# Full-width weight windows for the routing's counting and id products

## The chip, the core and the metric

The kernel runs on one core of one Trainium2 chip. Its time is the device time of one execution in microseconds (us), the median over several runs. A core has five engines with queues of their own: TensorE (PE in the profile; its weight loads are listed apart as PEld), VectorE (DVE), ScalarE (ACT), GpSimd (POOL) and SyncE (SP, which only issues transfers here). TensorE multiplies a stationary operand, which a weight load (LDWEIGHTS) brings into its array of 128 rows and 128 columns, with a moving operand, and writes the sums to PSUM.

## The reference

The input is the output of three layers, one after the other.

```python
attn = softmax(mask(q @ k.T / 8)) @ v        # 4 batches, 8 heads, 576 positions, window of 64 back
x = attn.reshape(2304, 512)

logits = x @ w_gate                          # 2304 tokens, 8 experts, cap = 288 per expert
for idx in np.argsort(-logits.flatten()):    # best pair of token and expert first
    tok, e = divmod(idx, 8)
    if assigned[tok] < 0 and counts[e] < 288:
        assigned[tok] = e; counts[e] += 1
y[mask_e] = relu(x[mask_e] @ w1[e]) @ w2[e]  # for each expert e

h = y @ w_in                                 # 512 -> 2048
out = maximum(0.01 * h, h) @ w_out           # 2048 -> 512
```

## The kernel before

Attention comes first (to about 87 us of the span). Then the greedy assignment is made in eight phases, 0 to 7, one for each expert that fills up. A phase looks for the logit at which the first expert reaches 288 tokens: six rounds of a search (r = 0 to 5) over the bits of the logit, each with J = 63 or 31 candidate thresholds. In a round VectorE compares each token's best logit with all candidates and writes the one-hot-like grid `GE` (128 partitions, 18 chunks of tokens, J columns, bf16). TensorE then counts: 18 small products, one per chunk, with `GE[:, c, :J]` stationary and the one-hot choice `OH[:, c]` (8 columns) moving, all adding into one PSUM tile `pc` with the counts of candidate j in row j. VectorE marks in `sat` which counts have reached the rest (`rem`), and one product with a constant 128x128 matrix `pow2[r]` sums the marked bits over the rows for all partitions. After the six rounds VectorE makes a running count (`W`, the scan `S`), two products with `tri` and `ones` turn it into positions, and 18 more products, with 36 columns of the grid `OB` stationary, give the list of token ids of this expert. So a phase has 6 x 18 counting products and 18 id products on TensorE; I call each such row of 18 a burst. Phase 7 has no search.

Phase 0 runs alone between attention and the first expert. Phases 1 to 6 are cut into small pieces and strewn among the products of the experts (tiles `h`, `ya`, moving 288 columns) and of the last two layers (tiles `h`, `oa`, moving 512 columns), in an order that a planner (`RouteDriver` with the cost table of `Clocks`) fixes when the program is built. Its cost of a product depends on the moving width alone. All these operations are issued through one helper, so the profile gives them one line, L1178; they are told apart by tile names: `rp<-r_oh,r_ge` is a counting product, `rp<-r_lo,r_ob` an id product, `rp<-r_sat,pow` the product behind a round, `rp<-r_tot` the two behind the scan.

The lines that matter (`start`/`stop` arguments left out; the first is in every round, the last at a phase's end):

```python
GE = t([128, NT, 64], BF, "ge", f"{ph}_{r}")
nc.tensor.matmul(pc[:J], GE[:, c, :J], OH[:, c, :])
TT(out=self.sat[:J], in0=pc[:J], in1=(self.rem0 if r == 0 else self.rem)[:J], op=ALU.is_ge)
nc.tensor.matmul(pa, self.pow2[r], self.sat)
nc.tensor.matmul(pi, OB[:, c, :2].rearrange("p a b -> p (a b)"), LO[:, c])
```

Of the kernel before, what the change touches and what calls it, by code (L numbers as in the profile page):

```python
# [58 lines left out]
def attention(nc, tc, ident, identb, qT, kT, v, vT, wg_sb, maskb, xd, L, filler, early, late, done):  # L59


    with ExitStack() as ctx:
# [208 lines left out]
def consts_np():  # L271

    f, i, b = {}, {}, {}
    p = np.arange(128, dtype=np.float32)[:, None]
    u = (np.arange(1, 64, dtype=np.uint64) << 26).astype(np.uint32)
    t = np.where(u >= 0x80000000, u ^ np.uint32(0x80000000), ~u).astype(np.uint32)
    i['t1'] = np.broadcast_to(t.view(np.int32), (128, 63))
    for r, (s, n) in enumerate(zip(SHIFTS, NB)):
        i[f'jt{r}'] = np.broadcast_to((np.arange(1, n + 1) << s).astype(np.int32), (128, n))
    f['ew'] = np.broadcast_to(8 - np.arange(8, dtype=np.float32), (128, 8))  # L280
    f['lim'] = np.where(p == 0, -1.0, 3e9).astype(np.float32)
    f['cid'] = np.broadcast_to(np.arange(18, dtype=np.float32), (128, 18))
    f['pid'] = np.broadcast_to(p, (128, 1))
    f['cont'] = np.broadcast_to((np.arange(288) % NT > 0).astype(np.float32), (128, 288))
    f['ident'] = np.eye(128, dtype=np.float32)
    j = np.arange(128)[:, None] % 18
    f['comb'] = (np.where(p < 18, 128, 1) * (j // 6 == np.arange(3))).astype(np.float32)
    b['mask'] = const_mask()
    b['ident'] = np.eye(128, dtype=np.float32)
    b['tri'] = (p < np.arange(128)[None, :]).astype(np.float32)  # L290
    b['iota'] = np.broadcast_to(np.arange(512, dtype=np.float32) % 128, (128, 512))
    b['spread'] = (j % 6 == np.arange(96) // 16).astype(np.float32)
    b = {k: (np.ascontiguousarray(a).view(np.uint32) >> 16).astype(np.uint16) for k, a in b.items()}
    return f, i, b
# [9 lines left out]
class Router:  # L304
# [3 lines left out]
    def __init__(self, nc, pool, pp, L, cf, ci, cb, ones_b, pow2):  # L308
        self.nc, self.pool, self.pp = nc, pool, pp
        self.cf, self.ci, self.tri, self.iota, self.ones, self.pow2 = cf, ci, cb['tri'], cb['iota'], ones_b, pow2  # L310
        self.Lm, self.nps = L, 0
        self.base = pool.tile([128, 2, 8], F32, name="r_base")
        self.uw = pool.tile([128, 8], F32, name="r_uw")
        self.slotg = pool.tile([128, NT], F32, name="r_slotg")
        self.rem = pool.tile([128, 8], F32, name="r_rem")
        self.rem0 = pool.tile([128, 8], F32, name="r_rem0")
        self.spread = cb['spread']
        self.sat = pool.tile([128, 8], BF, name="r_sat")
        self.ip = pool.tile([128, 128], F32, name="r_ip")
    def start(self):  # L320
        v, cf = self.nc.vector, self.cf
# [11 lines left out]
    def t(self, shape, dt, name, ph):  # L333
        bufs = {"fb": 2, "ns": 2, "T": 2, "U": 2, "ids": 8, "eidx": 8}.get(name, 1)
        return self.pool.tile(shape, dt, tag="r_" + name, name=f"r_{name}_{ph}", bufs=bufs)
    def ahead(self, a, b):

        v = self.nc.vector
        if a == 0:
            self.first = [self.t([128, NT], F32, "m", 0), self.t([128, NT, 8], BF, "oh", 0), self.t([128, NT], F32, "mxw", 0)]  # L340
            self.ge0 = self.t([128, NT, 64], BF, "ge", "0_0")
            self.eqw0 = self.t([128, NT, 8], F32, "eqw", 0)
        m, OH, mxw, eqw = self.first[0][:, a:b], self.first[1][:, a:b], self.first[2][:, a:b], self.eqw0[:, a:b]
        def b3(ap, last):
            return ap.unsqueeze(2).to_broadcast([128, b - a, last])
        def bm(ap, last):
            return ap.unsqueeze(1).to_broadcast([128, b - a, last])
        v.tensor_reduce(out=m, in_=self.Lm[:, a:b], axis=AX.X, op=ALU.max)
        yield True
        v.tensor_tensor(out=eqw, in0=self.Lm[:, a:b], in1=b3(m, 8), op=ALU.is_equal)  # L350
        yield True
        v.tensor_tensor(out=self.ge0[:, a:b, :63], in0=b3(m, 63), in1=bm(self.ci['t1'].bitcast(F32), 63), op=ALU.is_ge)
        v.tensor_tensor(out=eqw, in0=eqw, in1=bm(self.cf['ew'], 8), op=ALU.mult)
        yield True
        v.tensor_reduce(out=mxw, in_=eqw, axis=AX.X, op=ALU.max)
        yield True
        v.tensor_tensor(out=OH, in0=eqw, in1=b3(mxw, 8), op=ALU.is_equal)
    def phase(self, ph, out):

        nc, t = self.nc, self.t
        v, cf, ci = nc.vector, self.cf, self.ci
        Lm = self.Lm
        TT, TS, STT = v.tensor_tensor, v.tensor_scalar, v.scalar_tensor_tensor
# [4 lines left out]
        if ph:  # L370
# [8 lines left out]
            OH = t([128, NT, 8], BF, "oh", ph)  # L379
            TT(out=OH, in0=eqw, in1=b3(mxw, NT, 8), op=ALU.is_equal)  # L380
            yield 'd', 0
        else:
            m, OH, mxw = self.first
        theta = None
        if ph < 7:
            fb = ns = U = None
            T = ci['t1']
            for r in range(6):
                J = 63 if r == 0 else NB[r - 1]
                GE = self.ge0 if ph + r == 0 else t([128, NT, 64], BF, "ge", f"{ph}_{r}")  # L390
                pc = None
                for lo, hi in () if ph + r == 0 else ((0, 9), (9, 18)) if J > 32 or ph == 0 else ((0, 18),):
                    w = hi - lo
                    TT(out=GE[:, lo:hi, :J], in0=b3(m[:, lo:hi], w, J), in1=bm(T.bitcast(F32), w, J), op=ALU.is_ge)
                    if hi == 9:
                        yield 'p' if ph == 0 else 'd', 0
                        if ph == 0:
                            pc = self.ps(64, 8)
                            for c in range(9):
                                nc.tensor.matmul(pc[:J], GE[:, c, :J], OH[:, c, :], start=(c == 0), stop=False)  # L400
                if r >= 2:
                    nf = t([128, 1], I32, "fb", f"{ph}_{r}")
                    TT(out=nf, in0=fb, in1=ns, op=ALU.bitwise_xor)
# [4 lines left out]
                    TT(out=U[:, :Jn], in0=ci[f'jt{r}'], in1=fb.to_broadcast([128, Jn]), op=ALU.bitwise_xor)  # L408
                yield 'p', 0
                c0 = 9 if pc is not None else 0  # L410
                pc = self.ps(64, 8) if pc is None else pc
                for c in range(c0, NT):
                    nc.tensor.matmul(pc[:J], GE[:, c, :J], OH[:, c, :], start=(c == 0), stop=(c == NT - 1))
                yield 'v', 1
                TT(out=self.sat[:J], in0=pc[:J], in1=(self.rem0 if r == 0 else self.rem)[:J], op=ALU.is_ge)
                yield 'p', 0
                pa = self.ps(128, 8)
                nc.tensor.matmul(pa, self.pow2[r], self.sat, start=True, stop=True)
# [3 lines left out]
                if r == 0:  # L422
                    k = t([128, 2], I32, "k", ph)
# [13 lines left out]
        ge = t([128, 2, NT], F32, "gteq", ph)  # L437
# [4 lines left out]
        else:  # L442
# [2 lines left out]


        yield 'd', 0
        W = t([128, 2, 8, NT], BF, "ge", f"{ph}_W")
        TT(out=W, in0=OH.rearrange("p c e -> p e c").unsqueeze(1).to_broadcast([128, 2, 8, NT]),
           in1=ge.unsqueeze(2).to_broadcast([128, 2, 8, NT]), op=ALU.mult)  # L450
        S = t([128, 2, 8, NT], F32, "ob", f"{ph}_S")
        v.tensor_tensor_scan(S.rearrange("p k e c -> p (k e c)"), cf['cont'], W.rearrange("p k e c -> p (k e c)"), 0.0, ALU.mult, ALU.add)
        yield 'd', 0
        tot = t([128, 16], BF, "tot", ph)
        v.tensor_copy(tot.rearrange("p (k e) -> p k e", k=2), S[:, :, :, NT - 1])
# [49 lines left out]
        TS(out=hl[:, 0], in0=loc, scalar1=4, scalar2=None, op0=ALU.arith_shift_right)  # L505
        TS(out=hl[:, 1], in0=loc, scalar1=15, scalar2=None, op0=ALU.bitwise_and)
        yield 'd', 0
        OB = t([128, NT, 3, 18], BF, "ob", ph)
        LO = t([128, NT, 16], BF, "lo", ph)
        TT(out=OB[:, :, 2], in0=b3(hl[:, 0], NT, 18), in1=bm(self.iota[:, :18], NT, 18), op=ALU.is_equal)  # L510
        yield 'd', 0
# [2 lines left out]
        TT(out=OB[:, :, 0], in0=OB[:, :, 2], in1=b3(cf['cid'], NT, 18), op=ALU.mult)  # L514
        TS(out=OB[:, :, 1], in0=OB[:, :, 2], scalar1=cf['pid'], scalar2=None, op0=ALU.mult)
        yield 'p', 0
        pi = self.ps(36, 16)
        for c in range(NT):
            nc.tensor.matmul(pi, OB[:, c, :2].rearrange("p a b -> p (a b)"), LO[:, c], start=(c == 0), stop=(c == NT - 1))
        yield 'v', 1  # L520

        TT(out=self.ip[:36, :96].rearrange("p (a b) -> p a b", a=6), in0=pi.unsqueeze(1).to_broadcast([36, 6, 16]), in1=self.spread[:36].rearrange("p (a b) -> p a b", a=6), op=ALU.mult)
        yield 'p', 0
        pj = self.ps(128, 3)
        nc.tensor.matmul(pj, self.ip, cf['comb'], start=True, stop=True)
# [16 lines left out]
def make_pow2(nc, pool):  # L542
    out = []
    for r, (s, n) in enumerate(zip((25,) + SHIFTS, (63,) + NB)):
        w = pool.tile([128, 128], BF, name=f"pow2_{r}", tag=f"pow2_{r}")
        nc.gpsimd.memset(w, 0.0)
        nc.gpsimd.memset(w[:n], float(1 << s))
        out.append(w)
    return out

# [813 lines left out]
```

## Time and profile before

| what | value |
|---|---|
| time, median of 3 runs | 797.8 us (797.09 to 800.81) |
| time of the profiled execution | 801.13 us |
| span of its instructions | 798.9 us |
| TensorE busy | 757.1 us, 95% of the span |
| VectorE busy | 436.9 us, 55% |
| ScalarE busy | 340.4 us, 43% |
| share of the chain that ended last: TensorE | 60% |
| of it, products that write the tile `rp` | 4% |
| mean granted clock of TensorE | 0.975 of full speed |

The table is read from the page of the profile: its first part gives busy times, its fourth the chain of work that ended last, followed back from the end. Busy time of TensorE runs from the start of a product to its modelled end, so products that follow each other overlap, and what a product costs is seen in the distance between starts, not in its duration.

### The profile page before, as it was taken

To read this page: it belongs to the slowest core of one execution; us is meant where nothing else is said; L and a number is where in the kernel's file an instruction comes from. 1 tells how busy PE (TensorE), PEld (TensorE's weight loads), DVE (VectorE), ACT (ScalarE), POOL (GpSimd) and SP (SyncE) were. 2 spreads that over 40 slices of the span, in tenths; PEclk is the share of its full clock that TensorE was granted. 3 is DMA by queue.
4 is the path that set the end of the run, shared out by engine and by line. 5 is a ranking of instruction groups with operands and counts; after the bars stand their busy time and mean duration, and the time that the engine had idled before them with its cause. 6 is when DMAs were issued, how large, how long until landed. Compare 5 with 4: busy or idle time off the path is not lost.

```text
span 798.9 us, 15084 instructions
## 1 busy us (share of the span) xinstructions
PE 757.1 (95%) x5829; PEld 632.8 (79%) x5829; DVE 436.9 (55%) x1191; ACT 340.4 (43%) x754; POOL 143.0 (18%) x174
## 2 busy tenths in 40 slices
PE   6999659899999999999999999999999999999996
PEld 4777527689877789997777899988889998888895
DVE  3687775779798887977658434222223213222332
ACT  4798804578565544522111355321235532212221
POOL 3334020100100003010000186400017740000201
PEclk9999758999999999999999999999999999999999
DMA  9996144654685558473224286723337653124742
GB/s 344 409 410 231 55 150 155 217 224 84 211 288 160 211 187 172 157 173 114 105 80 159 80 188 206 219 80 125 117 128 184 165 180 134 66 93 158 255 168 106
DMA packets 44759, 138.72 MB, mean 174 GB/s; under 512 B 9742, under 2 KB 10638, under 8 KB 44688
## 3 DMA queue, kind: packets, MB, share of 16 engines
q1 hardware_dynamic: 40816, 126.39, 47.0%
q0 software_dynamic: 3440, 11.02, 5.5%
q8 instruction: 46, 0.75, 0.4%
q10 hardware_dynamic: 432, 0.36, 0.1%
q14 instruction: 25, 0.20, 0.1%
HBM read 117.81 MB, written 19.93 MB: 172 GB/s over the span
## 4 chain that ended last, share of the span: by engine, by line
PE 60%; issue 15%; DMA 11%; DVE 8%; ACT 4%; POOL 2%; POOLq 0%; SPq 0%; DVEq 0%; ACTq 0%
PE h L1178 26%; PE oa L1178 16%; PE ya L1178 9%; PE rp L1178 4%; DMA raw<-in_w_dram 3%; DMA avo<-in_v_dram 2%; DMA cv_in<-in_wio_dram 2%; PE ao L161 1%; PE apt L146 1%; DMA xg<-xd,r_ids 1%; ACT ap L141 1%; PE as L128 1%; POOL w L1178 1%; DMA sidx<-idl 1%; DVE w L1178 1%
## 5 line engine op out<-in xcount | busy, mean ns | idle before, releaser
L1178 PE MATMUL h<-Y,w 128*128 128x512 f32 (+1 forms) x600 | 138.4, 376 | 0.0
L1178 PE MATMUL oa<-w,hh 128*128 128x512 f32 x540 | 134.4, 394 | 0.0
L1178 ACT COPY tg<-h 128x512 f32<-128x512 f32 (+1 forms) x80 | 43.6, 545 | 197.9 <-PE h L1178 191.7
L1178 DVE SCALAR_TENSOR_TENSOR h<-h,tg 128x512 f32<-128x512 f32 (+1 forms) x80 | 51.6, 644 | 133.7 <-ACT tg L1178 133.4
L1178 PEld LDWEIGHTS h<-Y,w 128*128 128x128 f32 x600 | 104.4, 188 | 20.8
L1178 PEld LDWEIGHTS oa<-w,hh 128*128 128x128 f32 x540 | 99.6, 188 | 20.9
L1178 POOL TENSOR_TENSOR w<-raw,w 128x512 fp32r<-128x512 f32 x53 | 66.8, 1287 | 219.6 <-DVE xT L1178 110.7
L1178 PE MATMUL ya<-hh,w 128*128 128x288 f32 x672 | 102.5, 300 | 1.3 <-ACT hh L1178 0.8
L1178 PE MATMUL h<-xT,w 128*128 128x288 f32 x672 | 100.8, 298 | 0.0
L1178 PEld LDWEIGHTS ya<-hh,w 128*128 128x128 f32 x672 | 93.1, 190 | 3.8 <-ACT hh L1178 1.5
L1178 PEld LDWEIGHTS h<-xT,w 128*128 128x128 f32 x672 | 93.2, 189 | 0.7
L1178 PE MATMUL h<-Y,res 128*128 128x512 f32 (+1 forms) x360 | 82.5, 374 | 0.0
L1178 PE MATMUL oa<-res,hh 128*128 128x512 f32 x324 | 82.2, 398 | 0.0
L1178 PEld LDWEIGHTS h<-Y,res 128*128 128x128 f32 x360 | 62.6, 188 | 12.1
L1178 ACT CAST hh<-h 128x512 fp32r<-128x512 f32 (+1 forms) x80 | 43.5, 544 | 65.2 <-DVE h L1178 64.5
L1178 DVE TENSOR_TENSOR hh<-h,hh 128x512 fp32r<-128x512 f32 (+1 forms) x80 | 51.0, 637 | 36.7 <-ACT hh L1178 34.6
L1178 PEld LDWEIGHTS oa<-res,hh 128*128 128x128 f32 x324 | 59.6, 188 | 13.7 <-ACT hh L1178 0.3
L1178 ACT CAST w<-raw 128x512 fp32r<-128x512 f32 x112 | 64.0, 619 | 11.9 <-DMA raw<-in_w_dram 11.9
L1178 ACT ACTIVATE hh<-h 128x288 fp32r<-128x288 f32 (+1 forms) x64 | 26.5, 414 | 88.9 <-PE h L1178 88.2
L1178 DVE SCALAR_TENSOR_TENSOR hh<-h,hh 128x288 fp32r<-128x288 f32 x56 | 25.5, 455 | 66.1 <-ACT hh L1178 65.9
L1178 POOL DMA_INDIRECT out_dram<-ot,sidx x18 | 18.4, 1024 | 226.3 <-DVE ot L1178 134.6
L1178 POOL DMA_INDIRECT xg<-xd,r_ids x24 | 23.6, 983 | 136.9 <-DVE r_ac L1178 131.0
(160 smaller groups left out, 932.3 us busy)
## 6 DMA issues: line engine op xcount, KB each, us to landing
w<-wsp SPq DMA_DIRECT2D x80, 512.0 KB, 4.1
raw<-in_w_dram SPq DMA_DIRECT2D x61, 512.0 KB, 4.9
cv_in<-in_wio_dram SPq DMA_DIRECT2D x32, 512.0 KB, 5.9
wsp<-w SPq DMA_DIRECT2D x20, 512.0 KB, 3.5
avo<-in_v_dram SPq DMA_DIRECT2D x6, 876.0 KB, 10.1
aq<-in_q_dram SPq DMA_DIRECT2D x12, 384.0 KB, 9.4
avt<-in_vt_dram SPq DMA_DIRECT2D x6, 768.0 KB, 10.2
xd<-ax SPq DMA_DIRECT2D x18, 256.0 KB, 6.7
```

The source lines that it names most:

```text
L128: nc.tensor.matmul(S[64 * t:64 * t + 64, a, u, :].rearrange("p (b c) -> p b c", b=2), q[h], k[h], start=False, stop=True, skip_group_check ...
L141: nc.scalar.activation(p[:, u, :], S[:, a, u, :], AF.Exp, bias=nm[:, a, u:u + 1], scale=0.125)
L146: nc.tensor.transpose(pt[:, u, :], p[:, u, :], ident)
L161: nc.tensor.matmul(o[64 * t:64 * t + 64, h // 4, h % 4, :], ptb[:, u, 64 * t:64 * t + 64], (ve, vo)[t][m][:, s, h, :], start=True, stop=Tr ...
L1178: return f(*a, **kw)
```

## The change

The grid that VectorE writes gets a fixed home: two buffers `G[0]` and `G[1]` of 64 + 64 x 18 columns, used in turn by the rounds, set to zero once by GpSimd at the start. A chunk now has 64 or 32 columns (`w`), and the stationary operand of chunk c is no longer its own J columns but the window of 128 columns that ends with them, `G[:, w*c : w*c+128]`; the windows of neighbouring chunks overlap. The chunk's own counts therefore come out in the last rows of PSUM, from row 64 or 96 on, and `sat`, `lim` and `pow2` use those rows; the rows above hold sums over other chunks, which `pow2` multiplies by zero. The id products read windows of 128 columns of a fixed `OB` in the same way and use the first 36 rows of the result. `W` and `S` are laid into `G[0]` and `OB`. The constant `cont` moves from the float table `cf` to the bfloat16 table `cb`.

```diff
-    f['lim'] = np.where(p == 0, -1.0, 3e9).astype(np.float32)
+    f['lim'] = np.where(p == 64, -1.0, 3e9).astype(np.float32)
-    f['cont'] = np.broadcast_to((np.arange(288) % NT > 0).astype(np.float32), (128, 288))
+    b['cont'] = np.broadcast_to((np.arange(288) % NT > 0).astype(np.float32), (128, 288))
...
+        self.G = [pool.tile([128, 64 + 64 * NT], BF, name=f"r_G{k}") for k in range(2)]
+        self.OB = pool.tile([128, 1048], BF, name="r_OB")
+        for x in self.G + [self.OB]:
+            nc.gpsimd.memset(x, 0.0)
...
+    def grid(self, k, w):
+        f = 128 - w
+        return self.G[k][:, f:f + w * NT].rearrange("p (c j) -> p c j", j=w), lambda c: self.G[k][:, w * c:w * c + 128]
...
-                GE = self.ge0 if ph + r == 0 else t([128, NT, 64], BF, "ge", f"{ph}_{r}")
+                jw = 64 if J > 32 else 32
+                rows = slice(128 - jw, 128 - jw + J)
+                GE, win = (self.ge0, self.win0) if ph + r == 0 else self.grid(r % 2, jw)
...
-                    nc.tensor.matmul(pc[:J], GE[:, c, :J], OH[:, c, :], start=(c == 0), stop=(c == NT - 1))
+                    nc.tensor.matmul(pc, win(c), OH[:, c, :], start=(c == 0), stop=(c == NT - 1))
-                TT(out=self.sat[:J], in0=pc[:J], in1=(self.rem0 if r == 0 else self.rem)[:J], op=ALU.is_ge)
+                TT(out=self.sat[rows], in0=pc[rows], in1=(self.rem0 if r == 0 else self.rem)[rows], op=ALU.is_ge)
...
-        W = t([128, 2, 8, NT], BF, "ge", f"{ph}_W")
+        W = self.G[0][:, 64:64 + 16 * NT].rearrange("p (k e c) -> p k e c", k=2, e=8)
-        S = t([128, 2, 8, NT], F32, "ob", f"{ph}_S")
+        S = self.OB.bitcast(F32)[:, :16 * NT].rearrange("p (k e c) -> p k e c", k=2, e=8)
...
-        OB = t([128, NT, 3, 18], BF, "ob", ph)
+        OB = self.OB[:, :54 * NT].rearrange("p (c a b) -> p c a b", a=3, b=18)
...
-            nc.tensor.matmul(pi, OB[:, c, :2].rearrange("p a b -> p (a b)"), LO[:, c], start=(c == 0), stop=(c == NT - 1))
+            nc.tensor.matmul(pi, self.OB[:, 54 * c:54 * c + 128], LO[:, c], start=(c == 0), stop=(c == NT - 1))
...
-        nc.gpsimd.memset(w[:n], float(1 << s))
+        a = 64 if n > 32 else 96
+        nc.gpsimd.memset(w[a:a + n], float(1 << s))
```

Every engine issues the same operations in the same order as before, but for GpSimd. On TensorE, at the end of a burst of phase 2, where the products of expert 1 (tiles `h`, `ya`) go on, there stood:

```order
1235 L1178 LDWEIGHTS r_ge_2_2821
1236 L1178 MATMUL rp_2853<-r_oh_2584,r_ge_2_2821 31x8
1237 L1178 MATMUL h_2844<-xT_0_2646,w_11_2724 128x288
1238 L1178 MATMUL h_2844<-xT_1_2647,w_11_2724 128x288
1239 L1178 MATMUL h_2844<-xT_0_2646,w_11_2724 128x288 x2
1240 L1178 MATMUL h_2844<-xT_1_2647,w_11_2724 128x288
1241 L1178 MATMUL h_2844<-xT_0_2646,w_11_2724 128x288
1242 L1178 MATMUL ya_0_2745<-hh_2811,w_10_2726 128x288 x2
1243 L1178 LDWEIGHTS pow_2_96
```

and now there stands:

```order
1235 L1189 LDWEIGHTS r_G_114
1236 L1189 MATMUL rp_2838<-r_oh_2572,r_G_114 128x8
1237 L1189 MATMUL h_2829<-xT_0_2633,w_11_2710 128x288
1238 L1189 MATMUL h_2829<-xT_1_2634,w_11_2710 128x288
1239 L1189 MATMUL h_2829<-xT_0_2633,w_11_2710 128x288 x2
1240 L1189 MATMUL h_2829<-xT_1_2634,w_11_2710 128x288
1241 L1189 MATMUL h_2829<-xT_0_2633,w_11_2710 128x288
1242 L1189 MATMUL ya_0_2731<-hh_2797,w_10_2712 128x288 x2
1243 L1189 LDWEIGHTS pow_2_96
```

Nothing moved; the result has 128 rows where it had 31, and the weights come from the fixed buffer. On GpSimd, at the start of the program, before the first operation of attention there (tile `ave`), the rows were:

```order
13 L547 MEMSET pow_3_99 31x128
14 L546 MEMSET pow_4_102 128x128
15 L547 MEMSET pow_4_102 31x128
16 L546 MEMSET pow_5_105 128x128
17 L547 MEMSET pow_5_105 31x128
18 L100 MEMSET ave_229 64x584
19 L110 COPY ave_229<-avo_139 64x584
```

and are now:

```order
13 L558 MEMSET pow_3_99 31x128
14 L556 MEMSET pow_4_102 128x128
15 L558 MEMSET pow_4_102 31x128
16 L556 MEMSET pow_5_105 128x128
17 L558 MEMSET pow_5_105 31x128
18 L322 MEMSET r_G_114 128x1216
19 L322 MEMSET r_G_115 128x1216
20 L322 MEMSET r_OB 128x1048
21 L100 MEMSET ave_235 64x584
22 L110 COPY ave_235<-avo_145 64x584
```

Three memsets stand ahead of that of `ave`. The transfer of `cf` on ScalarE's queue shrinks from 447 to 159 columns of four bytes, that of `cb` on SP's grows from 736 to 1024 columns of two bytes.

## Rows read from the trace of the kernel before

**Rows 1.** The page: engines' busy time and instructions; GB/s in 40 slices.

```profile
PE 757.1 (95%) x5829; PEld 632.8 (79%) x5829; DVE 436.9 (55%) x1191; ACT 340.4 (43%) x754; POOL 143.0 (18%) x174
...
GB/s 344 409 410 231 55 150 155 217 224 84 211 288 160 211 187 172 157 173 114 105 80 159 80 188 206 219 80 125 117 128 184 165 180 134 66 93 158 255 168 106
```

**Rows 2.** By stage: PE, PEld, DVE, ACT, POOL busy; PEclk; DMA share; GB/s.

```profile
87.00:112.00 25.00, 8.23 (x151) 6.66 (x148) 18.63 (x86) 11.62 (x33) 1.15 (x2) 0.55 0.17 60
...
178.10:204.00 25.90, 25.59 (x227) 23.14 (x226) 23.90 (x79) 19.90 (x37) 0.00 (x0) 1.00 0.45 87
204.00:445.00 241.00, 239.02 (x1673) 196.04 (x1672) 190.40 (x553) 91.44 (x175) 13.35 (x17) 1.00 0.54 168
```

**Rows 3.** Weight loads by form: line, engine, operation, names, partitions*columns, xcount.

```profile
L1178 PEld LDWEIGHTS <-r_ge 128*31 128x31 bf16 x504 | 14.9, 96 | 12.8 <-DVE r_ge L1178 5.5 <-issue 2.8 <-DVE r_fb L1178 1.1
...
L1178 PEld LDWEIGHTS <-r_ge 128*63 128x63 bf16 x252 | 10.3, 120 | 9.4 <-DVE r_ge L1178 5.1 <-issue 2.4 <-DVE r_ge L352 1.2
...
L1178 PEld LDWEIGHTS <-r_ob 128*36 128x36 bf16 x144 | 4.3, 98 | 9.3 <-DVE r_ob L1178 7.8 <-DVE h L1178 0.7 <-DVE hh L1178 0.4
```

**Rows 4.** Timeline of PE, phase 3: start us, us, engine, line, operation, partitions*columns, xcount.

```profile
248.01 1.10 PE L1178 MATMUL h<-Y,res 128*128 128x512 f32 x4
249.04 0.61 PE L1178 MATMUL rp<-r_oh,r_ge 128*31 128x8 bf16 x18
249.58 2.12 PE L1178 MATMUL oa<-w,hh 128*128 128x512 f32 x8
251.54 0.18 PE L1178 MATMUL rp<-r_sat,pow 128*128 128x8 bf16 x1
251.58 1.16 PE L1178 MATMUL oa<-w,hh 128*128 128x512 f32 x4
252.58 0.40 PE L1178 MATMUL h<-Y,w 128*128 128x512 f32 x1
```

**Rows 5.** Timeline of PE around a 63-column burst of phase 6.

```profile
391.48 1.10 PE L1178 MATMUL h<-Y,w 128*128 128x512 f32 x4
392.51 0.75 PE L1178 MATMUL rp<-r_oh,r_ge 128*63 128x8 bf16 x18
393.18 0.97 PE L1178 MATMUL h<-Y,w 128*128 128x512 f32 x3
```

**Rows 6.** Timeline of PE, two single 128-column products of phase 4.

```profile
325.34 0.17 PE L1178 MATMUL rp<-r_tot,cbt 128*128 128x16 bf16 x1
325.37 0.17 PE L1178 MATMUL rp<-r_tot,ones 128*128 128x16 bf16 x1
```

**Rows 7.** Timeline of PE in phase 0.

```profile
91.97 1.30 PE L1178 MATMUL rp<-r_oh,r_ge 128*63 128x8 bf16 x18 [1.88 <-DVE r_ge L1178]
...
94.65 0.76 PE L1178 MATMUL rp<-r_oh,r_ge 128*31 128x8 bf16 x18 [0.97 <-DVE r_ge L1178]
...
104.87 0.17 PE L1178 MATMUL rp<-r_tot,cbt 128*128 128x16 bf16 x1 [2.56 <-DVE r_tot L1178]
104.89 0.17 PE L1178 MATMUL rp<-r_tot,ones 128*128 128x16 bf16 x1
```

**Rows 8.** Timeline of PE where attention ends and the first burst begins.

```profile
87.21 0.22 PE L161 MATMUL ao<-avo,aptb 128*64 128x73 f32 x1
87.27 0.69 PE L1178 MATMUL rp<-r_oh,r_ge 128*63 128x8 bf16 x17
```

**Rows 9.** Chain of waits, in order of time: start us, us, what.

```profile
136.31 6.76 DMA cv_in<-in_wio_dram
...
153.97 6.77 DMA xg<-xd,r_ids
...
165.47 6.88 DMA raw<-in_w_dram
```

**Rows 10.** Timeline of POOL at the start.

```profile
14.61 0.66 POOL L110 COPY ave<-avo 64x584 f32<-64x584 f32 x1 [10.67 <-DVE avo L108]
```

**Rows 11.** Chain of waits at the start.

```profile
14.11 9.88 DMA avo<-in_v_dram
```

More of the change, by code (lines that the diff above doesn't have):

```diff
@@ L316, in __init__ @@
         self.rem0 = pool.tile([128, 8], F32, name="r_rem0")
-        self.spread = cb['spread']
+        self.spread, self.cont = cb['spread'], cb['cont']
         self.sat = pool.tile([128, 8], BF, name="r_sat")
+        self.G = [pool.tile([128, 64 + 64 * NT], BF, name=f"r_G{k}") for k in range(2)]
+        self.OB = pool.tile([128, 1048], BF, name="r_OB")
+        for x in self.G + [self.OB]:
+            nc.gpsimd.memset(x, 0.0)
         self.ip = pool.tile([128, 128], F32, name="r_ip")
@@ L340, in ahead @@
             self.first = [self.t([128, NT], F32, "m", 0), self.t([128, NT, 8], BF, "oh", 0), self.t([128, NT], F32, "mxw", 0)]
-            self.ge0 = self.t([128, NT, 64], BF, "ge", "0_0")
+            self.ge0, self.win0 = self.grid(0, 64)
             self.eqw0 = self.t([128, NT, 8], F32, "eqw", 0)
@@ L397, in phase @@
                         if ph == 0:
-                            pc = self.ps(64, 8)
+                            pc = self.ps(128, 8)
                             for c in range(9):
-                                nc.tensor.matmul(pc[:J], GE[:, c, :J], OH[:, c, :], start=(c == 0), stop=False)
+                                nc.tensor.matmul(pc, win(c), OH[:, c, :], start=(c == 0), stop=False)
                 if r >= 2:
@@ L410, in phase @@
                 c0 = 9 if pc is not None else 0
-                pc = self.ps(64, 8) if pc is None else pc
+                pc = self.ps(128, 8) if pc is None else pc
                 for c in range(c0, NT):
-                    nc.tensor.matmul(pc[:J], GE[:, c, :J], OH[:, c, :], start=(c == 0), stop=(c == NT - 1))
+                    nc.tensor.matmul(pc, win(c), OH[:, c, :], start=(c == 0), stop=(c == NT - 1))
                 yield 'v', 1
-                TT(out=self.sat[:J], in0=pc[:J], in1=(self.rem0 if r == 0 else self.rem)[:J], op=ALU.is_ge)
+                TT(out=self.sat[rows], in0=pc[rows], in1=(self.rem0 if r == 0 else self.rem)[rows], op=ALU.is_ge)
                 yield 'p', 0
@@ L447, in phase @@
         yield 'd', 0
-        W = t([128, 2, 8, NT], BF, "ge", f"{ph}_W")
+        W = self.G[0][:, 64:64 + 16 * NT].rearrange("p (k e c) -> p k e c", k=2, e=8)
         TT(out=W, in0=OH.rearrange("p c e -> p e c").unsqueeze(1).to_broadcast([128, 2, 8, NT]),
            in1=ge.unsqueeze(2).to_broadcast([128, 2, 8, NT]), op=ALU.mult)
-        S = t([128, 2, 8, NT], F32, "ob", f"{ph}_S")
-        v.tensor_tensor_scan(S.rearrange("p k e c -> p (k e c)"), cf['cont'], W.rearrange("p k e c -> p (k e c)"), 0.0, ALU.mult, ALU.add)
+        S = self.OB.bitcast(F32)[:, :16 * NT].rearrange("p (k e c) -> p k e c", k=2, e=8)
+        v.tensor_tensor_scan(S.rearrange("p k e c -> p (k e c)"), self.cont, W.rearrange("p k e c -> p (k e c)"), 0.0, ALU.mult, ALU.add)
         yield 'd', 0
@@ L516, in phase @@
         yield 'p', 0
-        pi = self.ps(36, 16)
+        pi = self.ps(128, 16)
         for c in range(NT):
-            nc.tensor.matmul(pi, OB[:, c, :2].rearrange("p a b -> p (a b)"), LO[:, c], start=(c == 0), stop=(c == NT - 1))
+            nc.tensor.matmul(pi, self.OB[:, 54 * c:54 * c + 128], LO[:, c], start=(c == 0), stop=(c == NT - 1))
         yield 'v', 1
-        TT(out=self.ip[:36, :96].rearrange("p (a b) -> p a b", a=6), in0=pi.unsqueeze(1).to_broadcast([36, 6, 16]), in1=self.spread[:36].rearrange("p (a b) -> p a b", a=6), op=ALU.mult)
+        TT(out=self.ip[:36, :96].rearrange("p (a b) -> p a b", a=6), in0=pi[:36].unsqueeze(1).to_broadcast([36, 6, 16]), in1=self.spread[:36].rearrange("p (a b) -> p a b", a=6), op=ALU.mult)
         yield 'p', 0
```

## The prediction

> **What bounds the kernel now.** I read the busy times of the page first, then the busy time by stage, then the chain of waits, and last the timeline of TensorE around a few bursts. TensorE is busy 757.1 of 798.9 us, VectorE 436.9 [rows 1]. The stages differ. From 204 to 445 us, where phases 3 to 7 are strewn among the experts and the last layers, TensorE is busy 239.02 of 241 us and VectorE 190.40 [rows 2]: what a burst takes from TensorE there comes off the end one for one. From 178 to 204 us TensorE has 25.59 of 25.90 us, but VectorE has 23.90, so both are close to the bound [rows 2]. From 87 to 112 us, phase 0, TensorE is busy 8.23 of 25 us: the two engines wait for each other in a chain, and a shorter burst shortens the chain; the clock is the low one for most of it (granted 0.55 on average, of the levels 2.4 and 1.2 GHz) [rows 2]. Between 112 and 178 us the chain goes through transfers: one of 6.76 us from 136.31, a gather of 6.77 us from 153.97, expert weights of 6.88 us from 165.47 [rows 9]. A burst beside these is hidden; one ahead of them starts them sooner.
>
> **How many bursts.** 504 loads of 31 columns are 28 bursts of 18, 252 of 63 columns are 14, 144 of 36 columns are 8 [rows 3]. By the code phase 0 holds 4, 2 and 1 of them, phases 1 to 6 hold 4, 2 and 1 each, phase 7 one id burst.
>
> **What a burst costs now.** The product that follows without anything between starts (1.10 - 0.40) / 3 = 0.233 us after the one before [rows 4], where 0.40 is one product's duration. From the start at 248.01 to the start at 251.54 there are 12 such products and one burst of 31 columns: 3.53 - 12 x 0.233 = 0.73 us for the burst. Inside it the products are (0.61 - 0.17) / 17 = 0.026 us apart, 0.44 us in all [rows 4, 6], so some 0.3 us of the 0.73 is lost where the stream goes into the burst and out of it. The entry alone: four products start at 248.01, the burst at 249.04, which is 1.03 us instead of 4 x 0.233 = 0.93. The burst of 63 columns: from 391.48 to the third product after it, which starts at 393.18 + 0.97 - 0.40 = 393.75, lie six steps and the burst, 2.27 - 1.40 = 0.87 us, with (0.75 - 0.17) / 17 = 0.034 us inside [rows 5].
>
> **What a full-width product costs.** The product behind a round has 128 columns, the same type and 8 moving columns. Put alone into the same stream it takes, from 251.54 to the start of the fourth product after it (251.58 + 1.16 - 0.40 = 252.34), 0.80 - 3 x 0.233 = 0.10 us [rows 4]. So no 0.3 us are lost at its ends: what costs time there goes with the narrow form, not with the type. The first burst of all points the same way. It has 63 columns and follows attention's products of 64 columns, and starts 0.06 us after the last of them, without a gap [rows 8]. I read it as a price for changing the width that the array is set to. For a second full-width load right behind a first there are the two products behind the scan: 0.03 us apart at the full clock [rows 6], 0.02 us at the low one [rows 7], where 63 columns need (1.30 - 0.17) / 17 = 0.066 and 31 columns (0.76 - 0.17) / 17 = 0.035 [rows 7]. So 128 columns are not loaded more slowly than 31, and I take 0.026 at either clock.
>
> **A rule against the change.** The Trainium skill (TensorE: Matmul & The Clock Gate, section LDWEIGHTS (loading the stationary operand)) gives a load's time as columns / 1.2 ns, an estimate of 107 ns for 128 columns; by it the sum would be some 50 us longer than before. The same page (section Weight-path perf modes) says that loads of 128 columns that are not FP32 take a faster path, by which the sum below stands. The pairs of products agree with the second [rows 6, 7], but show one step each, not seventeen, and from a tile that starts on an even boundary.
>
> **The sum.** A new burst costs 0.10 + 17 x 0.026 = 0.54 us, whatever its columns were. That is 0.19 less than 31 columns and 0.33 less than 63; 36 columns I take like 31.
> - Bursts of 31 after phase 0: 24, one of them beside the transfer from 136.31; 23 x 0.19 = 4.4 us.
> - Bursts of 63 after phase 0: 12, three beside transfers (the first of phase 1 beside the gather for expert 0, both of phase 2 beside those from 153.97 and 165.47); 9 x 0.33 = 3.0.
> - Id bursts after phase 0: six at 0.19; that of phase 1 starts after a wait, so only its end gains, 0.1; together 1.2.
> - Phase 0, at the low clock: the second round 1.13 - 0.44 = 0.69, four rounds 0.59 - 0.44 = 0.15 each, the id burst taken the same; 1.4. Its first burst lies ahead of a wait and gives nothing.
> - VectorE keeps what it has: the same operations on the same elements, other addresses. Cost nothing; between 178 and 204 us, where it is nearly full, I count half of the four bursts, so 0.4 is taken off.
> - The three memsets of GpSimd: its next work after the first memsets comes at 14.61 us, after 10.67 us of idling [rows 10]. A copy of 584 columns there takes 0.66 us [rows 10], so three memsets of 1048 to 1216 columns are estimated at 4 us at most, well under the idling. Without that cover they would delay attention's first values by their length.
> - The transfers: `cf` loses 288 x 4 x 128 bytes = 147 KB, `cb` gains 74 KB. At the 409 GB/s of the early slices [rows 1] the net 74 KB are 0.18 us, and the chain at the start goes through a transfer (from 14.11, 9.88 us) [rows 11]. Between 0 and 0.4; I take 0.2.
> - A wait is added in one place, VectorE's first write of the grid behind the memsets; they are over tens of us before.
>
> 4.4 + 3.0 + 1.2 + 1.4 + 0.2 - 0.4 = 9.8 us. The profiled execution took 801.1 us, the median of the runs is 797.8; 801.1 - 9.8 = 791.3, and in the same ratio 797.8 becomes 788.0. Own range 785 to 791.5: the switch cost per burst is known to about 0.05 us over some 38 bursts (2 us), and the clock has stretches at the low level that need not fall alike.
>
> **Rivals.**
> 1. The width has nothing to do with the 0.3 us; it is the first load's wait for VectorE, which a burst keeps. The product behind a round waits only at its multiplication, its weight load waits for nothing, so the trace does not exclude this; the gapless first burst speaks against it [rows 8]. Left are the steps inside: 17 x (0.034 - 0.026) = 0.14 for 9 bursts, 1.2, with phase 0 and the transfers 2.8 us: 798.3, as a median 795.0.
> 2. TensorE gets its 0.19 to 0.33 us back but then waits for VectorE or a routing chain that has not become shorter. VectorE has room from 204 us on (190.40 of 241), which speaks against it; little room before. With half of the 8.6 us after phase 0 lost in this way 5.9 us remain: 795.2, as a median 791.9.
> 3. Slower: windows that overlap and start anywhere do not get the fast load, and 128 columns load at the rate of the 63. The step is then 0.034 x 128 / 63 = 0.069, a burst 0.10 + 17 x 0.069 = 1.27, that is 0.54 more than 31 or 36 columns (29.5 bursts, 15.9) and 0.40 more than 63 (9 bursts, 3.6). In phase 0 the steps become 0.066 x 128 / 63 = 0.135: 1.2 more in the second round, 1.7 in five others, 9.7. Together 29 us: 830, as a median 827. It decides from a step of about 0.037 at the full clock, where 0.19 / 17 = 0.011 more per step eats the gain of a 31-column burst. The two products 0.03 apart speak against it. The first rule of the Trainium skill above would be its harder form.
>
> **How the numbers follow.** The forecast gets 0.74, rival 1 0.12, rival 2 0.10, rival 3 0.04. A measurement of this kernel tells about 0.5% from no change, 4 us, so faster means below 793.8. That holds for the forecast nearly whole (0.72), for rival 2 mostly (0.09), for rival 1 in its lower part (0.03): 0.84. Within 0.5% lies the rest of rivals 1 and 2 and of the forecast, 0.12; slower is rival 3, 0.04. The range goes from 784.5, a little more gained per burst, up to 795, which takes in rival 2 and the middle of rival 1.
>
> **What would show it.** In the changed profile a burst between products of 512 columns should span some 0.6 us from its first start to the last end with 0.026 between starts, at both clocks; the product ahead of it should be followed after 0.24 us, not 0.33, and the whole burst should add about 0.54 us. The product counts stay. Phase 0 should be 1.4 us shorter, and the stage that now runs from 204 to 445 us about 6.5 us shorter with TensorE still over 98% busy. Wrong it would be if entry and exit stay as they are (rival 1), if TensorE shows new waits for VectorE (rival 2), or if the step inside rises above 0.037 (rival 3).

## The result, and the profile after

The changed kernel takes 787.06 us (median of four runs, 786.15 to 788.86) where the kernel before took 799.3 beside it (median of four, 797.09 to 802.52). The ratio is 0.985, interval 0.980 to 0.989: faster by 1.1 to 2.0%. A second set of runs on one chip, shown below, gave 0.988 (0.986 to 0.990). The profiled execution took 786.15 us, its span 784.3.

First the page's line of busy times, as in [rows 1]:

```profile
PE 743.7 (95%) x5829; PEld 625.1 (80%) x5829; DVE 440.3 (56%) x1191; ACT 340.5 (43%) x754; POOL 146.8 (19%) x177
```

TensorE has the same 5829 products and is busy 13.4 us less; VectorE has the same 1191 operations and about the same time. GpSimd has three more instructions. The weight loads by form (columns as in [rows 3]) show that the products are wider, not fewer:

```profile
L1189 PEld LDWEIGHTS <-r_G 128*128 128x128 bf16 x756 | 23.3, 97 | 18.8 <-DVE r_G L1189 11.4 <-issue 2.1 <-DVE r_G L356 1.2
L1189 PEld LDWEIGHTS <-r_OB 128*128 128x128 bf16 x144 | 4.2, 97 | 8.4 <-DVE r_OB L1189 7.3 <-issue 0.8 <-DVE hh L1189 0.3
```

756 is the 504 + 252 of before. A load of 128 columns has a mean of 97 ns here, one of 31 columns had 96, one of 63 had 120. These durations overlap each other, so a burst has to be read from the timeline. This is the same burst of phase 3 that [rows 4] show, in the same columns:

```profile
240.00 1.56 PE L1189 MATMUL h<-Y,res 128*128 128x512 f32 x6
241.40 0.61 PE L1189 MATMUL rp<-r_oh,r_G 128*128 128x8 bf16 x18
241.87 2.08 PE L1189 MATMUL oa<-w,hh 128*128 128x512 f32 x8
243.79 0.18 PE L1189 MATMUL rp<-r_sat,pow 128*128 128x8 bf16 x1
...
381.06 0.61 PE L1189 MATMUL rp<-r_oh,r_G 128*128 128x8 bf16 x18
```

Six products start in 241.40 - 240.00 = 1.40 us, which is 6 x 0.233: the stream no longer stops ahead of the burst. From 240.00 to the product at 243.79 lie 14 steps of 0.233 and the burst, 3.79 - 3.26 = 0.53 us for the burst, where [rows 4] gave 0.73. The last row is the burst of phase 6 that had 63 columns in [rows 5], where it was 0.75 us long: 0.61 us, as the others.

By stage, over the same windows as [rows 2]:

```profile
87.00:112.00 25.00, 7.94 (x130) 5.36 (x127) 18.95 (x87) 10.85 (x32) 2.12 (x3) 0.54 0.22 73
178.10:204.00 25.90, 25.29 (x196) 21.99 (x195) 24.01 (x78) 18.02 (x34) 1.62 (x2) 1.00 0.52 105
204.00:445.00 241.00, 238.90 (x1689) 198.31 (x1688) 190.77 (x545) 92.23 (x177) 15.44 (x19) 1.00 0.54 167
```

From 204 to 445 us TensorE is still 99% busy, so what the bursts gave up has come off the end. The trace as a whole was compared by setting each of the 5829 products against the same product of the kernel before. The table gives how much earlier a stretch lets TensorE go on (us; stretches by the times of before). The last three columns are experiments of the next section: e4_again, e1_narrow and e3_cont.

| stretch | predicted | changed | changed, again | windows narrow | only `cont` |
|---|---|---|---|---|---|
| start to 84.8, attention | 0.2 | 0.79 | 0.92 | 0.90 | 1.04 |
| to 116.4, phase 0 | 1.4 | 0.43 | 0.42 | 0.43 | 0.47 |
| to 204.5, phases 1 and 2 | 1.4 | 5.62 | 4.56 | 1.50 | 1.83 |
| to 442.8, phases 3 to 7 | 6.6 | 6.26 | 4.77 | 0.57 | -0.31 |
| to 792.0, end | 0.2 | 1.52 | 1.57 | 1.05 | 1.16 |

The last line says little of the change: 0.7 to 1.1 us of it lie between 610 and 668 us in all four columns, so they point to the profiled execution of before, 801.1 us, and not to an edit. The third line is disturbed by the clock. These are windows of before and then of the changed kernel (columns as in [rows 2]; the number before the last two is the granted clock):

```profile
120.00:126.80 6.80, 6.80 (x38) 4.49 (x38) 4.00 (x12) 2.03 (x4) 0.00 (x0) 0.50 0.51 181
174.60:178.00 3.40, 3.40 (x16) 3.40 (x16) 2.42 (x7) 3.37 (x7) 0.00 (x0) 0.50 0.25 93
```

```profile
119.60:123.00 3.40, 3.32 (x8) 2.07 (x9) 2.38 (x8) 0.00 (x0) 0.00 (x0) 0.50 0.87 319
123.00:126.40 3.40, 3.40 (x31) 2.64 (x31) 1.73 (x5) 2.95 (x6) 0.00 (x0) 1.00 0.03 13
174.60:178.00 3.40, 3.40 (x41) 3.20 (x40) 3.27 (x9) 3.31 (x7) 0.00 (x0) 1.00 0.56 155
```

Before, the granted clock was at the low level (0.50, 1.2 GHz) for 6.8 us from 120 and for 3.4 us from 174.6; in the changed kernel's execution for 3.4 us from 119.6 and not again until 781.8. The 6.8 us more at half speed are some 3.4 us of TensorE's work (an estimate: it is busy all through both windows of before). The execution "changed, again" has such stretches elsewhere; two of its windows:

```profile
170.40:173.80 3.40, 3.40 (x31) 3.25 (x30) 2.81 (x7) 3.40 (x6) 0.00 (x0) 0.50 0.00 0
228.40:231.80 3.40, 3.40 (x9) 2.33 (x8) 2.13 (x5) 1.24 (x2) 0.00 (x0) 0.50 0.98 364
```

Between the products at 231.3 and 242.9 us of before this execution loses 1.40 us where the other gains 0.18. Without that its 4.77 would be about 6.3, the changed kernel's 6.26.

### The profile page after: what moved, and what is told of

Its sections match the earlier page's. It is cut to its first block, busy times and chain, and to the rows that moved or that the text cites. A ratio compares the mean times of both kernels' runs of the same rounds, so it can differ in the third digit from the quotient of the medians.

```text
span 784.3 us, 15082 instructions
## 1 busy us (share of the span) xinstructions
PE 743.7 (95%) x5829; PEld 625.1 (80%) x5829; DVE 440.3 (56%) x1191; ACT 340.5 (43%) x754; POOL 146.8 (19%) x177
## 4 chain that ended last, share of the span: by engine, by line
PE 75%; DVE 10%; issue 5%; ACT 5%; DMA 4%; POOLq 0%; POOL 0%; DVEq 0%; ACTq 0%; SPq 0%
PE h L1189 33%; PE oa L1189 21%; PE ya L1189 11%; PE rp L1189 3%; PE apt L146 2%; PE ao L161 2%; PE as L128 2%; ACT ap L141 2%; DMA cv_in<-in_wio_dram 1%; DVE r_G L1189 1%; DVE w L1189 1%; DMA raw<-in_w_dram 1%; DVE r_OB L1189 1%; DVE cv_r L1189 1%; ACT cv_in L1189 1%
```

## The experiments

The first four ran on one chip, where the kernel before had a median of 798.89 us.

**e1_narrow: everything but the wide windows.** Each chunk's product reads only its own 31 or 63 columns of the fixed buffers, the id product 36, and the counts lie in the first rows. The memsets, the fixed buffers and the moved `cont` stay.

```diff
-        return ..., lambda c: self.G[k][:, w * c:w * c + 128]
+        return ..., lambda c, J: self.G[k][:, f + w * c:f + w * c + J]
...
-                rows = slice(128 - jw, 128 - jw + J)
+                rows = slice(0, J)
...
```

> The changed kernel with its fixed buffers, memsets, bfloat16 cont and smaller float table, but every counting product reads its own 63 or 31 columns and every id product its 36, results in the first rows as before. Theory (the array's width: going from full-width products to narrow ones and back costs time, and 63 columns load more slowly than 128): about 8.6 us of the gain after phase 0 go back, ratio to the kernel before 0.995 to 1.0, and in the trace a 31-column burst in the stream of 512-column products adds 0.73 us again, with entry 0.33 us. Rival (the gain comes from the fixed buffers, the transfers or the granted clock): stays at the changed kernel's time, ratio 0.985.

Measured: 795.63 us, ratio 0.997 (0.995 to 0.998). The timeline of the same burst:

```profile
243.60 2.34 PE L1188 MATMUL h<-Y,res 128*128 128x512 f32 x9
245.87 0.61 PE L1188 MATMUL rp<-r_oh,r_G 128*31 128x8 bf16 x18
246.40 2.11 PE L1188 MATMUL oa<-w,hh 128*128 128x512 f32 x8
248.36 0.18 PE L1188 MATMUL rp<-r_sat,pow 128*128 128x8 bf16 x1
```

The same nine products in the changed kernel:

```profile
239.22 2.34 PE L1189 MATMUL h<-Y,res 128*128 128x512 f32 x9
```

From their start to the burst it is 245.87 - 243.60 = 2.27 us here and 241.40 - 239.22 = 2.18 there; from the burst to the `pow` product behind it 2.49 here and 2.39 there. Those are 0.09 us at the entry and 0.10 behind it. Entry and exit cost again what they cost before, with the same VectorE operations and the same waits. So the 0.19 us belong to the narrow form. The single records show the same at nearly every burst from 204 us on: the product ahead of a burst is followed after 0.33 us here (0.24 in the changed kernel) when it has 512 columns, and the last counting product after 0.10 (0.025). Between this kernel and the changed one lie 795.63 - 788.86 = 6.8 us: the gain of the windows themselves, on one chip, where 8.6 were expected.

**e2_w127: windows one column short.** The counting products read 127 of the 128 columns; nothing else changes.

```diff
-        return ..., lambda c: self.G[k][:, w * c:w * c + 128]
+        return ..., lambda c: self.G[k][:, w * c:w * c + 127]
...
```

> The changed kernel with counting windows of 127 columns, the last column being one that is never used; id windows keep 128. Theory (two separate things: the width class of the array is still the full one, but the fast load needs all 128 columns): entry after a 512-column product stays near 0.24 us, the step inside a burst rises to about 0.069 us (0.034 x 128 / 63), a burst adds about 0.7 us more, and with some 34 bursts on the path the time is about 25 us longer than the changed kernel, near 812 us, slower than before. Rival (one thing only: any load above 64 columns is as fast as that of 128): 787 us, step 0.026. Rival (entry cost hangs on the load's kind and not on the width): entry 0.33 us and more.

Measured: 812.32 us, ratio 1.017 (1.015 to 1.020). Its timeline, a burst of phase 0 and that of phase 3:

```profile
91.05 2.09 PE L1189 MATMUL rp<-r_oh,r_G 128*127 128x8 bf16 x18 [1.87 <-DVE r_G L1189]
...
253.21 1.17 PE L1189 MATMUL rp<-r_oh,r_G 128*127 128x8 bf16 x18
254.24 2.07 PE L1189 MATMUL oa<-w,hh 128*128 128x512 f32 x8
```

The step inside is (1.17 - 0.17) / 17 = 0.059 us, against 0.026 for 128 columns; the rival of the slow load (0.069) is real and only one column away. Yet the stream enters this burst as it does one of 128 (the product ahead is followed after 0.23 us in the single records of the trace), and it leaves it after 0.059 us, one step, where 31 columns need 0.096 behind steps of 0.025. So two things are won by the change, and they are separate: no change of width, and the fast load. The Trainium skill (TensorE: Matmul & The Clock Gate, section Weight-path perf modes) ties the fast load to exactly 128 weights that are not FP32; both traces agree as to the 128; the type was not varied. At the low clock the step is 107 ns in the single records (the row of 2.09 us ends with a product of 0.25: (2.09 - 0.25) / 17 = 0.108), at the full one 59. The same page of the Trainium skill (section LDWEIGHTS) gives columns / 1.2 ns, an estimate of 106 ns for 127 columns; the trace agrees at the low clock alone.

**e3_cont: the kernel before with `cont` alone moved to the bfloat16 table.**

```diff
-    f['cont'] = np.broadcast_to((np.arange(288) % NT > 0).astype(np.float32), (128, 288))
+    b['cont'] = np.broadcast_to((np.arange(288) % NT > 0).astype(np.float32), (128, 288))
...
```

> The kernel before with one edit alone: the constant cont goes from the float table to the bfloat16 table, so 74 KB less are moved at the start and the float table lands sooner. Theory: 0.2 us, at most 0.8 us (attention's end lies 0.7 us earlier in the changed kernel's profile), ratio 0.999 to 1.0. Rival (the start carries a good part of the 12 us): ratio below 0.995.

Measured: 797.33 us, ratio 0.997 (0.995 to 0.999). Attention ends 1.04 us earlier, more than the 0.8 that was set as the most, and the ratio lies below the 0.999 to 1.0 of the theory, though its interval reaches there.

**e4_again: the changed kernel on the same chip.**

> The changed kernel once more, beside the others on the same chip. Theory: ratio 0.984 to 0.988, of which 9 to 10 us are the bursts and the rest the granted clock's low stretches, which differ between executions. Rival (the two profiles differ by 14.6 us of span and all of that is the change): ratio below 0.983.

Measured: 788.86 us, ratio 0.988 (0.986 to 0.990), 10.0 us below before. The larger gain that was set as the rival (below 0.983) is not seen.

The next four measure the disputed cost by itself: 192 idle products of 8 moving columns, strewn after every third product of 512 columns in the last groups of the second layer pair, with a stationary operand of 128, 127, 64 or 32 columns that is always ready (in the last group the products have 256 columns). Each ran once.

**x1_full, x2_127, x3_64, x4_32.**

```diff
+                if j % 3 == 2 and kind == 'm' and n >= 2:
+                    self.extra = getattr(self, 'extra', None) or self.route.r.ps(128, 8)
+                    nc.nc.tensor.matmul(self.extra[:128], self.warm[:, :128], self.warm[:, :8], start=True, stop=True, skip_group_check=True)
```

(in the others 127, 64 and 32 in place of 128)

> The changed kernel with 192 idle products put into the last three groups of the second layer pair, one behind every third product of 512 (in the last group 256) columns; each has 128 bf16 columns stationary and 8 moving, and its result is not used. Theory (one full-width product in this stream costs 0.10 us): 19 us longer than the changed kernel, about 806 us. Rival (a short product between long ones costs its own step alone, 0.026 us): 5 us, 792 us.

> The same with 127 columns. Theory (same width class, slower load, 0.059 instead of 0.025 us): 0.10 + 0.03 us each, about 25 us longer, 812 us. Rival (127 counts as narrow): as with 64 columns.

> The same with 64 columns. Theory (a change of the array's width on the way in and on the way out costs about 0.1 us each): 0.10 + 0.19 us each, about 56 us longer than the changed kernel, 843 us. Rival (the 0.3 us of a burst are its first load's wait for VectorE, which is not there here): as with 128 columns, 806 us.

> The same with 32 columns. Theory (the price is for leaving the full width, not for how narrow it gets): as with 64 columns, within 3 us. Rival (it grows with the number of parts the array is cut into): clearly longer than with 64.

Measured: 823.73, 818.92, 857.94 and 850.42 us; the kernel before took 808.0 in its one run beside them, some 9 us above its other runs on this chip, so the absolute numbers missed and the traces decide. One stretch of each timeline of TensorE, in the order 128, 127, 64, 32 (where "..." stands, the three products of 512 columns):

```profile
561.30 0.18 PE L877 MATMUL rp<-cbt 128*128 128x8 bf16 x1
561.34 0.95 PE L1192 MATMUL h<-Y,res 128*128 128x512 f32 x3
562.13 0.18 PE L877 MATMUL rp<-cbt 128*128 128x8 bf16 x1
```

```profile
559.83 0.17 PE L877 MATMUL rp<-cbt 128*127 128x8 bf16 x1
...
560.63 0.17 PE L877 MATMUL rp<-cbt 128*127 128x8 bf16 x1
```

```profile
559.44 0.19 PE L877 MATMUL rp<-cbt 128*64 128x8 bf16 x1
559.56 0.97 PE L1192 MATMUL h<-Y,w 128*128 128x512 f32 x3
560.46 0.19 PE L877 MATMUL rp<-cbt 128*64 128x8 bf16 x1
```

```profile
559.53 0.18 PE L877 MATMUL rp<-cbt 128*32 128x8 bf16 x1
...
560.53 0.18 PE L877 MATMUL rp<-cbt 128*32 128x8 bf16 x1
```

From one idle product to the next, with three products of 0.233 us between (0.70), lie 0.83, 0.80, 1.02 and 1.00 us, so 0.13, 0.10, 0.32 and 0.30 us go to an idle product. Over all 192 the stretch that holds them grew from 271.3 us to 295.3, 292.0, 332.1 and 329.4, that is 0.125, 0.108, 0.317 and 0.303 us each, or 24.0, 20.7, 60.8 and 58.1 us in all where 19, 25, 56 and 56 were expected: 127 columns came out cheaper than 128, not dearer. Leaving the full width for one product and coming back costs 0.19 us with 64 columns and 0.18 with 32, and no VectorE is in it. Rival 1 of the prediction is refuted by this as by e1_narrow. The Trainium skill (TensorEngine Tiling (Array Packing), section Key Properties) says that "Changing tiling mode (not just tile) drains the TensorE". The times agree with that if a product of 64 columns or fewer counts as another mode; that what is lost is a drain no row shows.

The last four ran on another chip, where before had a median of 806.23 us (801.3 to 811.5). They ask where the start's gain comes from, and whether a version can beat both kernels. The changed kernel itself was not run on this chip, so these versions are set beside it only by their ratios to before.

**y1_later: the kernel before, `cont` still float but in a later transfer of its own on SP's queue.**

```diff
-                nc.scalar.dma_start(cft, cfd)
+                nc.scalar.dma_start(cft[:, :159], cfd[:, :159])
...
+                nc.sync.dma_start(cft[:, 159:], cfd[:, 159:])
```

> The kernel before with the same bytes at the start, but cont (float, 147 KB) leaves the float table and gets a transfer of its own behind the other tables on SP's queue. Theory (the 0.8 to 1.0 us at the start come from the earlier landing of the float table, in whose way cont stood, since transfers issue in order): attention's end at about 86.3 to 86.5 us of the span, as in the run that only moved cont. Rival (they come from the 74 KB that are no longer moved): at 87.1 to 87.3, as before.

Measured: 807.3 us in one run; attention's last product starts at 87.63 us and the first burst at 87.69, where before it started at 87.27 [rows 8] (from another chip; y2_chip, on this one, has 86.83): later than either forecast, not earlier. A shorter first part of the float table is therefore not enough. But the extra transfer also moves others back on SP's queue, so bytes and place in the queue are not told apart.

**y2_chip: the changed kernel with `cont` made by two memsets of GpSimd, so that no table carries it.**

```diff
-    b['cont'] = np.broadcast_to((np.arange(288) % NT > 0).astype(np.float32), (128, 288))
...
+        nc.gpsimd.memset(self.cont, 1.0)
+        nc.gpsimd.memset(self.cont.rearrange("p (a c) -> p a c", c=NT)[:, :, 0:1], 0.0)
```

> The changed kernel with cont made on the chip by two memsets of GpSimd, so no table carries it (74 KB less than in the changed kernel). Theory (transfers bound attention's first 24 us, at some 400 GB/s): up to 0.2 us less than the changed kernel, ratio to the kernel before 0.986 to 0.989. Rival (the stage is no longer bound by transfers): no change against the changed kernel, 0.988.

Measured: 797.01 us, ratio 0.990 (0.986 to 0.994): no gain over the changed kernel is shown, with still fewer bytes; 0.2 us could not be told apart. Its chain at the start:

```profile
5.96 7.01 DMA avo<-in_v_dram
...
12.98 10.50 DMA avo<-in_v_dram
```

The transfer of `avo` ends the wait as in [rows 11], with 10.50 us against 9.88. In the changed kernel's own trace the chain of the start holds no `avo` at all:

```profile
1.65 4.54 DMA cbt<-in_cb_dram
...
6.24 1.03 PE as L119 x2
```

The second transfer of `avo`, which ends the wait in [rows 11], is issued at 14.11 us before and at 14.23 in y1_later, but at 13.23 in the changed kernel, 13.16 in e3_cont and 12.98 in y2_chip. For the changed kernel and e3_cont that is about what attention gains; in y2_chip part is lost again. How long the transfers of the first 24 us take is thus worth up to a microsecond and shifts from kernel to kernel by more than the 74 KB explain.

**y3_poollow: the changed kernel, and the low halves of expert weights may go to GpSimd in phase 2 too, to relieve VectorE between 178 and 204 us. y4_both: y2 and y3 together.**

```diff
-        return nc.gpsimd if self.ph >= 8 and ...
+        return nc.gpsimd if self.ph in (2, 8) and ...
```

> The changed kernel, whose planner may give the low halves of weights to GpSimd in phase 2 too (until now only after phase 7), which takes operations of 0.68 us off VectorE between about 165 and 204 us; the planner places the pieces around them anew. Theory (VectorE is the bound there, and hid the gain of that stage's bursts): 0.5 to 1.5 us less than the changed kernel, ratio 0.986. Rival (TensorE and VectorE wait for GpSimd's operations of 1.29 us): 1 us or more longer than the changed kernel, ratio 0.989 or above.

> The last two edits together. Theory: their gains add, ratio 0.985 to 0.988. Rival: as the changed kernel or worse, 0.988 or above.

Measured: 799.12 us, ratio 0.992 (0.989 to 0.995), and 800.15 us, 0.992 (0.989 to 0.995). No gain; the ratios lie where the rivals put them. The stage in y3_poollow, and then TensorE's waits in it (what waited, for what: us in total, times, longest); the planner has set the pieces anew, so the window holds fewer products than in the changed kernel:

```profile
178.10:204.00 25.90, 21.59 (x167) 20.27 (x167) 23.22 (x68) 13.20 (x27) 10.95 (x10) 0.93 0.43 67
```

```profile
PE rp L1189 <- DVE r_tot L1189: 2.4, 1, 2.4
PE rp L1189 <- DVE r_fb L1189: 1.6, 1, 1.6
PE rp L1189 <- DVE r_OB L1189: 0.3, 1, 0.3
```

GpSimd works 10.95 us there (1.62 in the changed kernel), but VectorE is hardly emptier (23.22 of 25.90) and TensorE now idles 4.3 us in waits for routing tiles that VectorE writes. By its ratio no version beat the changed kernel.

## Why the prediction was right, and which terms were off

The mechanism was right where most of the gain lies, at the bursts. That the total came out so near was in part luck: terms too high and terms too low cancelled, as the last paragraph of this section adds up.

**The burst: right.** Forecast were 0.54 us for any burst, a step of 0.026 at either clock, and a product ahead that is followed after 0.24 us. Measured are 0.53, 25 to 27 ns in the single records at both clocks (the first step of a burst is longer), and 0.23. The reading that decided it was the single full-width product of [rows 4], which fitted into the stream for 0.10 us, and the first burst of [rows 8], which starts without a gap because it has the width of attention's products. The changed kernel turns that case round: there the burst is wide and the products ahead are narrow.

```profile
86.43 0.22 PE L161 MATMUL ao<-avo,aptb 128*64 128x73 f32 x1
86.58 0.58 PE L1189 MATMUL rp<-r_oh,r_G 128*128 128x8 bf16 x17
...
91.19 0.40 PE L1189 MATMUL rp<-r_oh,r_G 128*128 128x8 bf16 x9 [1.88 <-DVE r_G L1189]
91.85 0.40 PE L1189 MATMUL rp<-r_oh,r_G 128*128 128x8 bf16 x9 [0.25 <-DVE r_G L1189]
...
93.64 0.76 PE L1189 MATMUL rp<-r_oh,r_G 128*128 128x8 bf16 x18 [0.97 <-DVE r_G L1189]
```

It starts 0.15 us after the last of them where it was 0.06: the price of the width now stands at this place.

**Where TensorE bounds: right.** From 204 us to the id burst at 442.8 the sum's terms give 6.6 us; the changed kernel gained 6.26 there. Taken from the second product ahead of each burst to the third behind it, the single records give 0.17 to 0.20 us at each of the 16 bursts that had 31 columns, 0.31 to 0.34 at seven of the eight that had 63, and 0.17 to 0.19 at four of the five id bursts; the 29 add up to 6.2 us, so the bursts are the stage's whole gain. It is about half of the whole gain, and nearly all of it is gone in e1_narrow (0.57).

**Phase 0: 1.4 us forecast, 0.3 gained by the windows.** The table's 0.43 and 0.42 hold these 0.3 us (up to 115 us, by the single products). The kernels without wide windows have 0.1 us or less up to there; their 0.43 and 0.47 come at the idle products `warm` after it, where the granted clock was already 1.00 in e1_narrow from 115 us and still 0.50 in the kernel before. The step that failed is the division (0.76 - 0.17) / 17 on [rows 7]. In phase 0 VectorE writes the grid in two halves and each burst is nine products, a wait, and nine more. The single records of before show 27 ns per step and one of about 125 between the halves; 0.035 was a mean across that wait. The row at 93.64 of the changed kernel is 0.76 us long as well: for 31 columns there was nothing to win inside at the low clock. For 63 columns the real step was 53 ns, and the products did get shorter, but the second half then waits for VectorE, as the rows at 91.19 and 91.85 show: from 1.30 us in [rows 7] to 91.85 + 0.40 - 91.19 = 1.06. The id burst, with 36 columns at 33 ns a step, gained 0.11. At the 63-column burst VectorE's writes of the two halves decide:

```profile
90.38 1.41 DVE L1189 TENSOR_TENSOR r_G<-r_m,r_T 128x567 bf16<-128x567 f32 x2
```

**From 178 to 204 us: 0.4 forecast, nothing gained.** Here rival 2 was true: I had left TensorE half of its gain, and waits took that as well, most of them for VectorE. The stage from the burst at 182.40 to the one at 204.47 takes 22.07 us in before and 22.22 in the changed kernel. Each of its bursts is shorter, but the time goes again behind them. Behind two, the `pow` product now waits for `sat`; before, then changed:

```profile
183.84 0.42 PE L1178 MATMUL ya<-hh,w 128*128 128x288 f32 x2
184.11 0.18 PE L1178 MATMUL rp<-r_sat,pow 128*128 128x8 bf16 x1
```

```profile
176.76 0.43 PE L1189 MATMUL ya<-hh,w 128*128 128x288 f32 x2
177.17 0.17 PE L1189 MATMUL rp<-r_sat,pow 128*128 128x8 bf16 x1
```

It starts 0.41 us after the products ahead of it, where it was 0.27; VectorE has written `sat` by 177.11. VectorE ahead of the next burst but one:

```profile
181.86 0.17 DVE L1189 TENSOR_REDUCE r_ns<-rp 128x1 int32<-128x8 f32 x1
182.06 0.19 DVE L1189 TENSOR_TENSOR r_T<-r_U,r_ns 128x31 int32<-128x31 int32 x1
182.28 0.74 DVE L1189 TENSOR_TENSOR r_G<-r_m,r_T 128x558 bf16<-128x558 f32 x1
...
183.01 0.45 DVE L1189 SCALAR_TENSOR_TENSOR hh<-h,hh 128x288 fp32r<-128x288 f32 x1
```

There is no idle time of VectorE among these; `r_G` ends at 183.02 and the burst starts at 183.08. Behind the scan TensorE then waits 0.29 us for `r_tot` from VectorE. In e4_again `pow` waits no longer than before, but 0.30 us go for `r_tot` and 0.48 for `hh` from ScalarE. TensorE's busy 25.29 of 25.90 hides these short waits.

**The start: 0.2 us forecast, 0.8 to 1.0 gained.** The mechanism, a smaller transfer ahead of the one that attention waits for, was right in sign; the size was not bytes over rate (0.18 us), the step of the sum that failed here. Moving `cont` alone gave 1.04, and taking it off altogether (y2_chip) gave no more. In the whole time e1_narrow is worth 3.3 us and e3_cont 1.6 by their medians, both with intervals of 1.4 us or more to each side; what e1_narrow has beyond the start's 0.9 us is not explained. Which of the first transfers is the one is open too.

**Phases 1 and 2: 1.4 us forecast for the stretch to 204.5 us, 5.6 and 4.6 gained.** Part is the granted clock, shown above. The execution e4_again and e1_narrow have their low stretches at nearly the same places there, and their difference is 4.56 - 1.50 = 3.1 us, still 1.7 above the forecast. Some 0.9 of that lies in one transfer on the chain of waits, `cv_in`, which takes 4.93 us in e4_again and 5.80 in e1_narrow (6.76 before [rows 9]); why it differs is open, and the rest was not settled.

**The memsets: right.** They run while GpSimd had nothing to do:

```profile
4.01 2.16 POOL L322 MEMSET r_G<- 128x1216 bf16 x2
```

With the third, 0.97 us, that is 3.1 us (4 at most was forecast), over by 7.1 us, well before the copy that [rows 10] show.

So the sum of 9.8 us was near the 10.0 and 12.2 measured partly by luck: phase 0 was set about 1 us too high and the start and phases 1 and 2 too low. The windows alone measured 6.8 where 9.6 were forecast for them, and the kernel without wide windows 3.3 where 0.2 were. Rival 3, slower, was refuted for 128 columns and shown for 127.

## What to carry to other kernels

When small products are strewn into a stream of full-width ones, give them 128 columns of bfloat16 even if most of the result is not used: the stream then doesn't pay for the change of width (0.19 us per visit here), and the loads keep the fast rate that 127 columns lose. Look for the price in the products before and after the burst, not in the burst's own rows. Where a burst is divided by a wait, take the step from single starts on one side of the wait, and count no gain for a burst whose next work VectorE still has to write.

## What the runs showed that was not expected

- The cost of the change of width hardly depends on how narrow the product is: an idle product took 0.303 us with 32 columns and 0.317 with 64, against 0.125 with 128. 127 columns don't pay it (0.108); where between 64 and 127 it ends was not tried.
- Alone among wide products 127 columns are a little cheaper than 128 (0.108 against 0.125 us), though in a burst they are more than twice as dear per step (0.059 against 0.026).
- At the low clock 128 columns and 31 columns both step at 27 ns (25 at the full one), while 63 columns go from 33 to 53 and 127 from 59 to 107: the fast load of 128 does not slow with the clock as the loads of 63 and 127 do.
- Two executions of one kernel have their low-clock stretches at different places; the one at 228.4 us cost about 1.6 us where TensorE bounds. One profile against another can show that much without any cause in the change.
